# Issuing the stores of k and z from ScalarE instead of from the sync queue

## The chip, the cores and the metric

The kernel runs on one core of a Trainium2 chip. A core has five engines that run their own instruction streams in order: TensorE (PE, with its weight loads PEld), VectorE (DVE), ScalarE (ACT), GpSimd (POOL) and SyncE (SP). SP, ACT and POOL can issue DMAs; 16 DMA engines carry them. The metric is the device time of one execution in microseconds (us), lower is better. Times are the median of several runs; the profile is of one more execution.

## The reference

The input x has shape (8, 3136, 256), in float32. The first block is the real part of a two-dimensional Fourier transform over sequence and features; the second is an MLP with a SoLU activation and a layer norm, over all 25088 tokens.

```python
X = np.fft.fft(x, axis=1)
X = np.fft.fft(X, axis=2)
x = X.real.reshape(B * S, D)
h = x @ w_in                                   # 256 -> 1024
e = np.exp(h - h.max(-1, keepdims=True))
solu = h * e / (e.sum(-1, keepdims=True) + 1e-9)
mu, var = solu.mean(-1, keepdims=True), solu.var(-1, keepdims=True)
out = ((solu - mu) / np.sqrt(var + 1e-6) * g_ln) @ w_out   # 1024 -> 256
```

## The kernel before

**The transform.** The sequence of 3136 is taken as 49 x 64. Batches go in four pairs. For each pair, `load` brings x and its mirrored rows (an indirect DMA from POOL), `add_mirror` and `fold` use the symmetry, and `transform1` does the transform over 49 on PE. ScalarE copies its result from PSUM into z (L154); after every second of these copies a store takes z to a DRAM scratch zd (L156), 8 stores a pair. `turn` reads zd back in another order as g, by four DMAs from POOL each time (L163). `transform2` (L174, L176) does the transform over 64 for one frequency k1, and `take2` copies the result into q (L182).

**Units.** A unit is one k1 of one pair; there are 25 per pair, 100 in all. A unit makes 128 rows of the output for k1 and, by symmetry, 128 for the mirrored frequency 49-k1; both are called signs, 0 and 1 (the first unit of a pair has sign 0 alone). In a unit: `up` multiplies q by the first weight (PE, L200); `even` and `join` make h and its maximum (VectorE); `expo` takes the exponential (ScalarE, L225); `product` multiplies (VectorE, L233) and POOL makes the negative mean (L235); `square` sums the squares (ScalarE, L242); `turn_blocks` transposes u in blocks of 32 x 32 into v (VectorE, L269); `stats` makes the scale (POOL).

**Moves.** The blocks must also change places between partitions. `move_blocks` does that with 16 DMAs on the sync queue, from v to uT (L278), once for a *batch* of two units, at the end of its odd unit. v and uT have two buffers each. This document calls them moves 0 to 15 of a batch; batch n has units 2n and 2n+1.

**Down and store.** `down` multiplies uT with the second weight (PE, L284), three units later (`lag = 3`): the first unit of batch n is multiplied in unit 2n+3, the second in 2n+4. It reads what all 16 moves write. ScalarE scales the result into ot (L290, four buffers). The rows of sign 0, the *store of k*, go out by a plain DMA (L296), those of sign 1 by an indirect DMA from POOL (L293).

**Order.** The loop over units is written by hand, and each engine and queue runs its instructions in that order. PE has up, transform2 of the next unit, transform1 of the next pair (units 4 to 19 of a pair, in the first three pairs), and down. ScalarE has q of the next unit, exp, z (if there is one), squares, ot. The sync queue has, at the end of an odd unit, the store of k of the old unit and then the 16 moves, then loads of x; z's store is issued in between, in units with odd k1.

**Completion counters.** The framework adds the waits. For DMAs issued by SP and ACT it keeps eight completion counters, DMAHW0 to DMAHW7, and gives them out in turn, in the one planned order in which it lists the instructions of all engines. A DMA waits until the DMA that had its counter before has landed.

The lines of the loop that set the order:

```python
            if old:
                store(old, 0, ps_o[0])
            if cur:
                if last:
                    move_blocks(batch, slice(cur.w, cur.w + 1))
                elif cur.w:
                    move_blocks(batch, slice(0, 2))
                stats(cur)
            if ahd:
                ahead(ahd, cur.k1)
            if old and 1 in old.signs:
                store(old, 1, ps_o[1])
```

Of the kernel before, what the change touches and what calls it, by code (L numbers as in the profile page):

```python
# [23 lines left out]
CH = 4  # L24
# [9 lines left out]
def kernel(  # L34
# [19 lines left out]
    nc = tc.nc  # L54
# [9 lines left out]
    out_k = out.rearrange("(p k2 k1) d -> p k1 k2 d", p=NP, k1=N1)  # L64
# [68 lines left out]
    def transform1(pr, s):  # L133

        c, l = divmod(2 * s, CH)
        if s == 0:
            pr.zd = dram.tile([ZR, NH, D], FP32, tag="zd", name="zd")
        if l == 0:  # L140
            pr.z = zpool.tile([ZR, CH, D], FP32, tag="z", name="z")
        y = pr.y[c]
        ps = ps_m.tile([P, 2, D], FP32, tag="m", name="ps1")
        if s == NH // 2 - 1:
            parts = [(ps[0:ZR, 0], y[:, l], 0), (ps[0:ZR, 1], pr.y0[:, 0], 1), (ps[0:ZR, 1], y[:, l + 1], 2)]
        else:
            parts = [(ps[0:ZR], y[:, l : l + 2], 0)]
        first = True
        for o, i, t in parts:
            for h, cs in enumerate((EVEN, ODD)):  # L150
                nc.tensor.matmul(o[..., cs], F[:, 2 * t + h, :], i[..., cs], start=first, stop=True,  # L151
                                 skip_group_check=True)
                first = False
        nc.scalar.copy(pr.z[:, l : l + 2, :], ps[0:ZR])  # L154
        if l == CH - 2:
            nc.sync.dma_start(out=pr.zd[:, c * CH : (c + 1) * CH, :], in_=pr.z)  # L156

    def turn(pr, i):

# [127 lines left out]
    def store(t, s, ps):  # L287

        ot = fpool.tile([P, D], FP32, tag="ot", name="ot", bufs=4)
        nc.scalar.mul(out=ot, in_=ps, mul=t.rs[:, s : s + 1])  # L290
        if s:
            i = NP * NC + t.p * (NK - 1) + t.k1 - 1
            dma = nc.gpsimd.indirect_dma_start(  # L293
                out=out, out_offset=bass.IndirectOffsetOnAxis(ap=idx[:, i : i + 1], axis=0), in_=ot, in_offset=None)
        else:
            dma = nc.sync.dma_start(out=out_k[t.p, t.k1], in_=ot)  # L296

        tc.declare_no_dep(dma.ins, group=f"out{1 - s}", reason="other rows of the output")
        tc.add_to_no_dep_group(f"out{s}", dma.ins)
# [106 lines left out]
    def ahead_pe(pr, step):  # L406

        if 0 <= step - 4 < NH // 2:
            transform1(pr, step - 4)
        elif step - 4 >= NH // 2:  # L410
            turn(pr, step - 4 - NH // 2)

    with tc.manual_schedule():
# [18 lines left out]
        for i in range(len(units) + lag):  # L432
# [26 lines left out]
            if old:  # L459
                store(old, 0, ps_o[0])  # L460
# [8 lines left out]
            if old and 1 in old.signs:  # L469
                store(old, 1, ps_o[1])  # L470
# [76 lines left out]
```

## Time and profile before

| | |
|---|---|
| median of 3 runs | 1433.51 us (1429.29 to 1437.84) |
| profiled execution | 1439.43 us, span 1437.7 us |
| mean granted TensorE clock | 0.923 |
| matmuls busy | 1234.3 us, 86% of the span |
| VectorE, ScalarE, GpSimd busy | 960.4, 615.1, 557.0 us |
| SP's and GpSimd's DMA queues | 58.1% and 9.9% of 16 engines' span |
| ScalarE's DMA queue | 1.7% |

The span is the profiled time from the first to the last instruction. "Busy" leaves out waits and the issuing of DMAs. Of a group of instructions the profile gives line, engine, operation, tiles and count, then the busy time and the mean duration in ns, then the idle time of the engine before them with what ended most of it. A name with a q (SPq) is an engine's sequencer, which waits and issues DMAs. In the list of waits each line has who waited, for whom, the microseconds in total, how often and the longest. In the timeline each line has start, duration, engine, line, operation and how many were merged.

### The profile page before, as it was taken

Reading aid. Unit: us, or ns where it says so; the run is one execution under the profiler, and the core shown is the slowest. Engines: PE = TensorE matmul, PEld = TensorE weight load, DVE = VectorE, ACT = ScalarE, POOL = GpSimd, SP = SyncE. Lnnn points to the kernel's source line nnn. Section 1 sums busy time; section 2 is a strip of 40 time slices with the busy share of each in tenths; the row PEclk is TensorE's granted clock in tenths of the full one; section 3 lists DMA queues with packets and bytes.
Section 4 is the critical chain, followed back from the end, with each engine's and each line's share of the span. In section 5 each row is a group of like instructions: output and inputs, shape, how many; then the busy total and the mean of one; then the engine's idle time right before and its main releaser. Section 6 shows DMA issues by size and latency. Waiting matters only on the chain.

```text
span 1437.7 us, 15866 instructions
## 1 busy us (share of the span) xinstructions
PE 1234.3 (86%) x4864; PEld 929.4 (65%) x4864; DVE 960.4 (67%) x1481; ACT 615.1 (43%) x1149; POOL 557.0 (39%) x972
## 2 busy tenths in 40 slices
PE   1633599999988899999977999999998898898888
PEld 1412376767766677777755777767676576776667
DVE  2597877667765767777656667767765856675671
ACT  1100445445543545554434355545543544454452
POOL 3430435444343444443344345444442323332331
PEclk9566899999999999999989999999999899999998
DMA  9640497795878758786688597886868557465564
GB/s 246 200 97 0 84 159 153 143 166 114 147 147 149 146 122 162 157 158 118 137 142 162 89 171 140 152 153 123 153 125 140 94 97 120 83 113 101 103 116 89
DMA packets 464628, 189.53 MB, mean 132 GB/s; under 512 B 433206, under 2 KB 446782, under 8 KB 464288
## 3 DMA queue, kind: packets, MB, share of 16 engines
q1 hardware_dynamic: 444752, 144.45, 58.1%
q0 software_dynamic: 13824, 38.55, 9.9%
q10 hardware_dynamic: 5968, 5.52, 1.7%
q8 instruction: 40, 0.66, 0.2%
q14 instruction: 44, 0.36, 0.1%
HBM read 44.78 MB, written 38.80 MB: 58 GB/s over the span
## 4 chain that ended last, share of the span: by engine, by line
PE 58%; SPq 15%; DVE 10%; DMA 9%; ACT 3%; issue 3%; POOL 2%; POOLq 0%; DVEq 0%; ACTq 0%
PE ps_o L284 37%; PE ps_h L200 16%; SPq L278 15%; DMA out_dram<-ot 4%; DMA uT<-v 3%; DVE h L214 2%; PE ps L151 2%; DMA xa<-in_x_dram 2%; DVE ex L312 2%; PE ps L174 2%; ACT h L242 1%; ACT u L225 1%; DVE u L233 1%; POOL nmean L235 1%; DMA xb<-in_x_dram,idx 1%
## 5 line engine op out<-in xcount | busy, mean ns | idle before, releaser
L284 PE MATMUL ps_o<-Wo,uT 128*128 128x256 f32 x3136 | 743.5, 398 | 100.4 <-DMA out_dram<-ot 58.1
L284 PEld LDWEIGHTS ps_o<-Wo,uT 128*128 128x128 f32 x3136 | 641.1, 206 | 181.9 <-issue 107.8
L200 PE MATMUL ps_h<-Wi,q 128*128 128x512 f32 x800 | 363.4, 597 | 7.4 <-DVE ev L206 6.4
L233 DVE SCALAR_TENSOR_TENSOR u<-h,u 128x1024 f32<-128x1024 f32 x196 | 232.5, 1223 | 139.2 <-ACT u L225 139.2
L235 POOL TENSOR_SCALAR nmean<-usum 128x1 f32<-128x1 f32 x196 | 128.7, 657 | 505.1 <-DVE u L233 504.9
L225 ACT ACTIVATE u<-h,neg 128x1024 f32<-128x1024 f32 x196 | 223.5, 1141 | 192.9 <-DVE neg L219 192.9
L242 ACT ACTIVATE h<-u,nmean 128x1024 f32<-128x1024 f32 x196 | 223.8, 1143 | 124.3 <-POOL nmean L235 124.3
L214 DVE CUSTOM_DVE_ANT_0 h<-ev,ps_h 128x1024 f32<-128x1024 f32 x196 | 231.7, 1219 | 50.4 <-PE ps_h L200 49.4
L206 DVE SCALAR_TENSOR_TENSOR ev<-w_mid,q,ps_h 128x1024 f32<-128x1024 f32 x100 | 127.8, 1278 | 202.4 <-PE ps_h L200 202.1
L200 PEld LDWEIGHTS ps_h<-Wi,q 128*128 128x128 f32 x800 | 152.8, 191 | 157.8 <-issue 148.4
L269 DVE STREAM_TRANSPOSE v<-u 128x1024 f32<-128x1024 f32 x200 | 238.5, 1234 | 0.1
L182 ACT COPY q<-ps 128x257 f32<-128x257 f32 x100 | 37.4, 374 | 257.7 <-PE ps L176 254.9
L293 POOL DMA_INDIRECT out_dram<-ot,idx x96 | 103.1, 1074 | 113.1 <-ACT ot L290 91.1
L290 ACT ACTIVATE ot<-ps_o,rs 128x256 f32<-128x256 f32 x196 | 83.6, 460 | 121.1 <-PE ps_o L284 121.1
L151 PE MATMUL ps<-y,F 98*100 98x258 f32 (+3 forms) x288 | 81.7, 424 | 42.4 <-DVE y L113 42.4
L254 POOL TENSOR_SCALAR v<-ssq 128x2 f32<-128x2 f32 (+1 forms) x100 | 27.8, 278 | 169.7 <-ACT h L242 169.7
L174 PEld LDWEIGHTS ps<-T,g 128*128 128x128 f32 x400 | 60.4, 191 | 47.4 <-issue 47.4
L151 PEld LDWEIGHTS ps<-y,F 98*100 98x100 f32 x288 | 48.7, 193 | 56.4 <-DVE y L113 25.5
L120 POOL TENSOR_TENSOR xa<-xa,xb 98x1020 f32<-98x1020 f32 (+1 forms) x32 | 72.8, 2274 | 25.4 <-DMA xa<-in_x_dram 16.7
L257 POOL TENSOR_TENSOR rs<-v,neg_half 128x2 f32<-128x2 f32 (+1 forms) x100 | 72.1, 721 | 7.8
L174 PE MATMUL ps<-T,g 128*128 128x128 f32 x400 | 60.7, 274 | 0.0
L163 POOL DMA_DIRECT2D g<-zd x80 | 47.9, 608 | 20.6 <-DMA zd<-z 11.6
(53 smaller groups left out, 492.9 us busy)
## 6 DMA issues: line engine op xcount, KB each, us to landing
uT<-v SPq DMA_DIRECT2D x784, 128.0 KB
zd<-z SPq DMA_DIRECT2D x32, 400.0 KB
g<-zd POOLq DMA_DIRECT2D x80, 160.0 KB, 5.1
out_dram<-ot SPq DMA_DIRECT2D x100, 128.0 KB
xa<-in_x_dram SPq DMA_DIRECT2D x32, 392.0 KB
raw_in_moe_w_in_dram<-in_moe_w_in_dram ACTq DMA_DIRECT2D x1, 2048.0 KB
raw_in_moe_w_out_dram<-in_moe_w_out_dram ACTq DMA_DIRECT2D x1, 2048.0 KB
uT<-v SPq DMA_DIRECT2D x32, 64.0 KB
```

Source lines behind the costliest of these rows:

```text
L151: nc.tensor.matmul(o[..., cs], F[:, 2 * t + h, :], i[..., cs], start=first, stop=True, skip_group_check=True)
L174: nc.tensor.matmul(ps[:, h * P : (h + 1) * P], g[:, k, h * P : (h + 1) * P], T[:, k1, :], start=(h == 0), stop=True, skip_group_check=True)
L200: nc.tensor.matmul(ps[:, fs], t.q[:, c * P : (c + 1) * P], Wi[:, c, fs], start=True, stop=True)
L206: nc.vector.scalar_tensor_tensor(out=t.ev, in0=w_mid, scalar=t.q[:, KD * P :], in1=ps, op0=ALU.mult, op1=ALU.add)
L214: nc.vector.tensor_tensor_reduce(out=t.h[s], in0=t.ev, in1=ps, scale=1.0, scalar=-3.0e38, op0=ALU.subtract if s else ALU.add, op1=ALU.max, ...
L225: nc.scalar.activation(out=t.u[s], in_=t.h[s], func=ACT.Exp, bias=t.neg[:, s : s + 1], accum_out=t.esum[:, s : s + 1])
L233: nc.vector.scalar_tensor_tensor(out=t.u[s], in0=t.h[s], scalar=1.0, in1=t.u[s], op0=ALU.mult, op1=ALU.mult, accum_out=t.usum[:, s : s + 1])
L235: nc.gpsimd.tensor_scalar(out=t.nmean[:, s : s + 1], in0=t.usum[:, s : s + 1], scalar1=-1.0 / FF, scalar2=None, op0=ALU.mult)
L242: nc.scalar.activation(out=t.h[s], in_=t.u[s], func=ACT.Square, bias=t.nmean[:, s : s + 1], accum_out=t.ssq[:, s : s + 1])
L269: nc.vector.transpose(out=t.batch.v[:, t.w, :, o], in_=t.u[s])
L278: nc.sync.dma_start(out=uT[b, i], in_=v[a, q])
L284: nc.tensor.matmul(ps, uT[:, c, :, s], Wo[:, c, :], start=(c == 0), stop=(c == KF - 1))
```

## The change

The two stores are issued by ScalarE's queue, each directly behind the ScalarE instruction that makes its data: z's store behind the copy of z, and the store of k behind the scaling into ot. Nothing else is edited. The engines' compute instructions and POOL's DMAs keep their order; 32 stores of z and 100 stores of k leave the sync queue, which keeps the moves and the loads of x.

```diff
         nc.scalar.copy(pr.z[:, l : l + 2, :], ps[0:ZR])
         if l == CH - 2:
-            nc.sync.dma_start(out=pr.zd[:, c * CH : (c + 1) * CH, :], in_=pr.z)
+            nc.scalar.dma_start(out=pr.zd[:, c * CH : (c + 1) * CH, :], in_=pr.z)
...
         else:
-            dma = nc.sync.dma_start(out=out_k[t.p, t.k1], in_=ot)
+            dma = nc.scalar.dma_start(out=out_k[t.p, t.k1], in_=ot)
```

## The prediction

> **What bounds the kernel now.** I read the page's shares first: TensorE (PE) is busy 86% of the span, VectorE 67%, ScalarE (ACT) 43%. Then the costliest groups and the chain that ended last:
>
> ```profile
> PE 1234.3 (86%) x4864; PEld 929.4 (65%) x4864; DVE 960.4 (67%) x1481; ACT 615.1 (43%) x1149; POOL 557.0 (39%) x972
> ...
> PE 58%; SPq 15%; DVE 10%; DMA 9%; ACT 3%; issue 3%; POOL 2%; POOLq 0%; DVEq 0%; ACTq 0%
> ...
> L284 PE MATMUL ps_o<-Wo,uT 128*128 128x256 f32 x3136 | 743.5, 398 | 100.4 <-DMA out_dram<-ot 58.1
> ```
>
> PE rules, but before its down matmuls (L284) it stands idle 100.4 us, and SP's issuing of moves is on the chain. The SP queue's own waits name what holds it:
>
> ```profile
> SPq L296 <- ACT ot L290: 388.8, 61, 12.9
> SPq L156 <- ACT z L154: 106.4, 21, 7.9
> SPq L278 <- DVE v L269: 88.5, 1, 88.5
> ```
>
> SP waits for ot 61 times and, after the first batch, never for v: at odd units the store of k stands ahead of the batch's 16 moves and holds them. The timeline shows one batch, SP first, then PE:
>
> ```profile
> 1282.36 0.34 SPq L296 DMA_DIRECT2D out_dram<-ot  x1
> 1282.80 13.74 SPq L278 DMA_DIRECT2D uT<-v  x16
> 1296.65 10.86 SPq L296 DMA_DIRECT2D out_dram<-ot  x2
> 1307.61 13.09 SPq L278 DMA_DIRECT2D uT<-v  x16
> ...
> 1291.39 3.60 PE L200 MATMUL ps_h<-Wi,q 128*128 128x512 f32 x8
> ...
> 1300.27 9.82 PE L284 MATMUL ps_o<-Wo,uT 128*128 128x256 f32 x32 [4.72 <-issue]
> 1309.92 3.60 PE L200 MATMUL ps_h<-Wi,q 128*128 128x512 f32 x8
> ...
> 1313.94 7.16 PE L284 MATMUL ps_o<-Wo,uT 128*128 128x256 f32 x32
> 1320.94 3.60 PE L200 MATMUL ps_h<-Wi,q 128*128 128x512 f32 x8
> ```
>
> I write U for the start of a unit's up (L200). An undisturbed unit takes 11.0 us (1309.92 to 1320.94) and down begins at U+4.0. With transform1 in the unit (16 of the 25 units of three pairs) these are 11.85 and 4.9 (timeline around 268 us). The batch of units 2n and 2n+1 is transposed by U+12.4 of its odd unit (1269.36 to 1281.80), stored k leaves at U+13.0, moves at U+13.4, and PE wants uT in the next odd unit, at U+22.0+4.0. Moves need about 16 us to land, so PE comes 3 to 5 us early in about every second batch, and the cold array then takes 9.8 instead of 7.2 us. Wait and cold time together I call the batch's excess. Period of two units less 22.0 (23.7 with transform1) gives it now: 3.9 us in the last pair (U 1034.6 to 1372.0, 13 batches), 1.5 in the first and third pairs' transform1 stretches (175.4 us for 7, 202.3 for 8), 0.8 in the second's (171.8 for 7), 4.5 in the nine batches between.
>
> **What the Trainium skill says.** DMA: Bandwidth & Descriptors, "Issuing engines are not separate DMA queues": other issuers use the same 16 engines and save only the sequencer's time. The page agrees that bytes don't change; SP's ring has 58.1%. Same page, "Why a DMA increments its semaphore by 16 and not by 1": only the full count says that data landed. Perfetto Trace Analysis, "DMA Instruction — HWDGE (DVE, Sync)": the descriptor generator is locked for one DMA, and its sequencer is free afterwards. No stretch of this trace has ACT issue small stores beside SP's moves. TensorE: Matmul & The Clock Gate, "What's actually happening": after an idle window of about 3.4 us the array runs at half rate; the 9.82 beside 7.16 us agrees.
>
> **What decides it: eight completion counters.** The program as built gives hardware DMAs (SP's and ACT's together) eight counters in turn, in the framework's planned order over all engines; a DMA waits until the one before it on its counter has *landed*. On one queue such a wait is on something issued earlier on the same queue. With k on ACT the planned order interleaves, and a move takes a counter from a store. From the changed program, batch 3 (third row is SP's move 13 of 0..15):
>
> ```
> ACT L290 Activation ot_1265<-ps_o_1236,rs_1012 128x256 [waits DMAHW7_49,PE_49]
> ACT L296 DMACopy out_0_dram<-ot_1265 128x256 [waits DMAHW3_49,Activation_49]
> SP  L278 DMACopy uT_1026<-v32_1025 32x16x64 [waits DMAHW3_49]
> ```
>
> ot_1265 is made in the *even* unit after the batch's odd unit, a whole unit after its v. So the last moves of each batch wait for that store: from move 13 or 14 on in batches 1-8, 13, 19, 24-33, and move 15 alone in the rest (9-12, 14-18, 20-23, 34-48). Before, that store simply queued behind the moves.
>
> **The change part by part.** *Removed:* SP's hold at odd units, 0.9 us (U+13.4 against U+12.45), up to 4 us more where ot itself was late. SP loses 132 issues of about 0.35 us, no cover needed.
> *Added on ACT:* 100 stores x 0.36 us and 32 z stores x 0.31 us (SP's own median durations) = 46 us. Covers: ACT idles 254.9 us before q over 93 waits, 2.7 each; h waits 124.3 us for nmean, which hides z. Behind a k store stand ot of sign 1, q and the next exp; q is ready at U+15.4, exp at U+17.5, ACT is through with the first two at U+13.8. So 0 us, until a store holds ACT beyond about 3.5 us.
> *Moved past other queues:* z leaves SP and meets the same cover; its landing of 3.6 us delays the next batch's first move by about the 1 us that was won, where a counter ties them. POOL keeps its order. In the prologue every load still waits for its fold (x loads leave at 38.5, 40.0, 46.2, 52.5, as folds end): 0.
> *Added wait, the largest term.* In the even unit, starting U': store leaves U'+13.0, lands after L, then the gated moves, then PE 0.25 later. L is not shown for ACT. The landing records of SP's k stores give 1.71 us (median, rings empty) and 3.9 (behind moves); I take 2.0, as the earlier moves have mostly landed by then. A move lands 2.66 us after its issue into empty rings, 3.7 to 4.1 in a train; I take 2.9, for the scatter of k's mirror is under way. Three gated moves add two issues of 0.62.
> Sum for one gated move: 13.0+2.0+2.9+0.25 = U'+18.15. PE wants it at 11.0+4.0 = U'+15.0 (11.85+4.9 = 16.75 with transform1). Waits: 3.15 us without transform1; 1.4 with it; 2.65 with it and three gated moves. Cold time after such waits, from the down durations of before (none up to 1.7 us, 1.3 on average near 2.3, 2.5 from 3.9): 1.7, 0.2, 1.4. New excess against old: 4.85-3.9 = 0.95 x 14 batches = 13; 4.05-1.5 = 2.55 x 16 = 41; 1.6-0.8 = 0.8 x 8 = 6; the nine others 4.85-4.5 = 0.35 x 9 = 3. Sum +63 us.
> Both ends: with 1.71 and 2.66 the waits are 2.6, 0.9, 2.1 and the sum about +20 us; with 3.9 and 4.1 they are 6.2, 4.5, 5.7 and the sum about +260. What is late next: the whole following unit, since up stands behind down on PE; the wait repeats in every batch, where now it comes in every second one.
>
> The profiled execution took 1439.4 us (span 1437.7); +63 makes 1502. The median shown, 1433.5, is 0.4% below the profiled one, so I forecast 1495.
>
> **Rivals.** *Freed moves win.* Moves start with v and land at U+12.45+16 = U+28.5. PE wants them at U+26.0 without transform1 (a wait of 2.5 us in one batch of two or 1.3 in each, with cold time an excess near 1.7) and at U+28.6 with it (none): 2.2 x 14 + 1.5 x 16 + 0.8 x 8 + 2.8 x 9 = 86 us less, 1350 us; half of it 1390. For it: 388.8 us of SP's waits vanish. Against: from U'+13.0 to U'+15.0 only 2.0 us remain for a store and a move that take 4.4 into empty rings. It decides only if the last moves don't wait for the store's landing.
> *ACT is held.* A store meets SP's 16 moves and the locked generator. One move's turn (0.6 to 0.9 us) hides. Beyond 3.5 us exp, v and the moves are late: a hold of 5 us costs 1.5 x 48 = 72 us more, 1565 us. For it: T's issues held ACT 8.3 and 5.1 us in the prologue. Against: those have 1600 small rows, k has 128.
> *Nothing measurable:* gains at odd units equal losses at even ones, 1434 us. It needs less than the +20 us of empty rings.
>
> **How the numbers follow.** About 0.5%, 7 us, is what a measurement of this kernel can tell from no change. Gated last moves, likeliest: 0.64, its own range 1450 to 1570. ACT held: 0.13. Freed moves: 0.13. Nothing: 0.10, of which I give 0.02 to slower. So faster 0.13, same 0.08, slower 0.79. The range 1420 to 1580 leaves out most of the full win below (0.09) and the worst of landing times and holds above (0.10).
>
> **What would show it.** Right: SP's waits for ot at L296 are gone, and SP waits 2 to 4 us per batch at L278 for a landing of out_dram<-ot; the train of moves begins within 0.2 us of v, and has a gap before its last one or three; L284's idle time rises from 100 to about 130 or more, with more durations near 9 us; ACT's k stores stay below 1.3 us. Wrong: an unbroken train of moves (freed moves), or ACT's issues of several us with u<-h late behind q (ACT held). The prediction fails most easily on the landing time of a store on ACT's ring: each us is about 45 us of the whole.

## The result and the profile after

The changed kernel takes 1522.26 us (median, 1518.97 to 1527.91), the kernel before, run beside it, 1435.67 us (1429.29 to 1439.85). The ratio is 1.0611 with the interval [1.0558, 1.0664]. The profiled span is 1517.2 us against 1437.7, which is 79.5 us more. The forecast was 1495 us, 1420 to 1580, slower.

The page of the changed kernel first: busy shares, the chain that ended last by engine, and down's group, which has its idle time behind the second bar.

```profile
PE 1252.8 (83%) x4864; PEld 940.4 (62%) x4864; DVE 964.5 (64%) x1481; ACT 624.0 (41%) x1149; POOL 556.8 (37%) x972
...
PE 53%; DVE 15%; DMA 13%; issue 7%; ACT 5%; SPq 4%; POOL 2%; DVEq 0%; POOLq 0%; ACTq 0%
...
L284 PE MATMUL ps_o<-Wo,uT 128*128 128x256 f32 x3136 | 764.1, 406 | 158.4 <-DMA uT<-v 80.1
```

PE's matmuls are busy 18.5 us longer and stand 58.0 us longer ahead of down (158.4 against 100.4); these two make 76.5 of the 79.5 us. The busy times of VectorE, ScalarE and GpSimd moved by less than 10 us each. SPq has fallen from 15% of the chain to 4%: SP no longer issues late, but what it waits for lands late. Its waits (for whom, sum, times, longest):

```profile
SPq L278 <- DVE v L269: 365.9, 37, 96.1
SPq L278 <- DMA out_dram<-ot: 216.7, 44, 9.1
SPq L278 <- DMA zd<-z: 121.4, 17, 11.5
```

The 388.8 us of waiting for ot at L296 are gone. Moves now wait for v, as one would wish; but 44 times a move waits until a store of k has landed, and 17 times until a store of z has. The timeline shows such a batch of the last pair: SP's first fifteen moves, ScalarE's store of k in the even unit, the sixteenth move (move 15), and on PE the start of the even unit, the start of the next and down.

```profile
1327.97 13.14 SPq L278 DMA_DIRECT2D uT<-v  x15
...
1342.28 0.34 ACTq L296 DMA_DIRECT2D out_dram<-ot  x1
...
1344.01 0.58 SPq L278 DMA_DIRECT2D uT<-v  x1
...
1329.34 3.60 PE L200 MATMUL ps_h<-Wi,q 128*128 128x512 f32 x8
...
1340.36 3.60 PE L200 MATMUL ps_h<-Wi,q 128*128 128x512 f32 x8
...
1347.15 8.84 PE L284 MATMUL ps_o<-Wo,uT 128*128 128x256 f32 x32 [2.63 <-issue]
1355.83 3.60 PE L200 MATMUL ps_h<-Wi,q 128*128 128x512 f32 x8
```

The even unit began at U' = 1329.34. Its store left at U'+12.93 and landed, by the landing records, at 1343.88, 1.61 us later. Move 15 was issued at 1344.01 and landed at 1346.95; PE began at 1347.15, after 2.63 us of waiting, and then ran down in 8.84 instead of 7.16 us. Before the change PE waited like this in about every second batch; now it does in nearly every one. The trace shows the cause in all of them: in batches 1 to 48 a late move has its counter from the even unit's store, in 40 of them it leaves within 0.06 us of that store's landing (seven of the other eight lie in the second pair, where z holds moves too), and in all 48 the landing of move 15 is the last of the batch, 0.1 to 0.5 us before down begins.

### The profile page after: what moved, and what is told of

Same layout as the page of the kernel before. It is cut to its first block, busy times and chain, and to the rows that moved or that the text cites. A ratio compares the mean times of both kernels' runs of the same rounds, so it can differ in the third digit from the quotient of the medians.

```text
span 1517.2 us, 15758 instructions
## 1 busy us (share of the span) xinstructions
PE 1252.8 (83%) x4864; PEld 940.4 (62%) x4864; DVE 964.5 (64%) x1481; ACT 624.0 (41%) x1149; POOL 556.8 (37%) x972
## 4 chain that ended last, share of the span: by engine, by line
PE 53%; DVE 15%; DMA 13%; issue 7%; ACT 5%; SPq 4%; POOL 2%; DVEq 0%; POOLq 0%; ACTq 0%
PE ps_o L284 36%; PE ps_h L200 15%; DMA uT<-v 7%; DVE h L214 6%; SPq L278 4%; DMA out_dram<-ot 2%; DVE u L233 2%; ACT u L225 2%; ACT h L242 2%; DMA xa<-in_x_dram 2%; DVE ex L312 2%; DMA zd<-z 2%; POOL nmean L235 1%; PE ps L174 1%; PE ps L151 1%
## 5 line engine op out<-in xcount | busy, mean ns | idle before, releaser
L284 PE MATMUL ps_o<-Wo,uT 128*128 128x256 f32 x3136 | 764.1, 406 | 158.4 <-DMA uT<-v 80.1
L284 PEld LDWEIGHTS ps_o<-Wo,uT 128*128 128x128 f32 x3136 | 653.4, 210 | 250.0 <-issue 141.8
L290 ACT ACTIVATE ot<-ps_o,rs 128x256 f32<-128x256 f32 x196 | 91.4, 466 | 201.6 <-PE ps_o L284 152.0
L151 PE MATMUL ps<-y,F 98*100 98x258 f32 (+3 forms) x288 | 77.5, 408 | 44.6 <-DVE y L113 44.6
L163 POOL DMA_DIRECT2D g<-zd x80 | 47.3, 603 | 13.6 <-issue 13.4
```

Source lines behind the costliest of these rows:

```text
L284: nc.tensor.matmul(ps, uT[:, c, :, s], Wo[:, c, :], start=(c == 0), stop=(c == KF - 1))
```

## The experiments

Ratios are to the kernel before, measured beside each version. "Batch n waits" is PE's idle time directly before down of unit 2n; its sum over 49 batches is 100.4 us before and 154.3 us in the changed kernel. The theory is that of the prediction: a move waits for the landing of a store that has the same completion counter (*tie*). The rivals are that issuing costs ScalarE or the rings time of its own, and that z is to blame rather than k.

**One store at a time.** Only k on ScalarE:

```diff
-            dma = nc.sync.dma_start(out=out_k[t.p, t.k1], in_=ot)
+            dma = nc.scalar.dma_start(out=out_k[t.p, t.k1], in_=ot)
```

> The stores of k alone on ScalarE's queue; z stays on the sync queue. Counter theory (a move waits for the landing of the store that had its completion counter): in the built program the store of k made in the even unit gives its counter to move 14 in batches 2 to 9 and 27 to 34 and to move 14 or 15 in nearly all others, so PE waits 2 to 3 us in each batch as in the changed kernel: 1495 to 1525 us, and SP waits some 200 us for landings of out_dram. Rival (the cost is what ScalarE pays for issuing, in proportion to stores): 100 of 132 stores, three quarters of the 87 us lost, about 1500 us. The two agree here; this run only tells whether z matters.

1512.79 us, ratio 1.0525 [1.0486, 1.0564]; the waits sum to 153.3 us.

```profile
SPq L278 <- DMA out_dram<-ot: 273.6, 55, 9.5
```

The stores of k make nearly all of the loss. With z the ratio is 1.0611 [1.0558, 1.0664], so z adds some 9 us, with intervals that just overlap. Only z on ScalarE:

```diff
-            nc.sync.dma_start(out=pr.zd[:, c * CH : (c + 1) * CH, :], in_=pr.z)
+            nc.scalar.dma_start(out=pr.zd[:, c * CH : (c + 1) * CH, :], in_=pr.z)
```

> The stores of z alone on ScalarE's queue; k stays on the sync queue. Counter theory: the planned order is another one, and in it move 15 of batches 2 to 8 and 27 to 33 (and 14 of 26) takes its counter from the z store of the very unit whose down reads the batch. That store is issued 9.2 us after the unit's up starts, lands 3.6 later, the move 2.9 later, and PE wants it at 4.9: a wait of about 11 us and 2.5 cold in 15 batches, some 12 us more than before in each, 180 in all; moves 11 to 15 of batches 14 to 20 wait for z in the even unit, some 15 us more. About 1630 us (1580 to 1680). Rival (ScalarE pays for issuing, in proportion to stores): 32 of 132 stores, about 1456 us; and if ScalarE's idle time covers them, 1436.

1650.54 us, ratio 1.151 [1.1474, 1.1545]: half of the change costs more than twice as much as the whole. In the program as built, move 15 of batches 2 to 8 and 27 to 33 then has its counter from the z that is stored in the very unit in which PE wants the batch, and these batches wait 10.3 to 11.3 us each. SP's waits show both what stayed and what came:

```profile
SPq L296 <- ACT ot L290: 456.6, 61, 11.6
SPq L278 <- DMA zd<-z: 275.2, 24, 15.2
```

The two edits don't add up, because each shifts which DMAs share a counter. No account by work on engines gives this size: 32 issues of 0.31 us moved from one queue to another.

**Stores of k by the unit in which they are made.** The changed kernel, with the stores of odd units and z still on ScalarE and the stores of even units back on the sync queue:

```diff
+            odd = (t.p * NK + t.k1 + 3) % 2
-            dma = nc.scalar.dma_start(out=out_k[t.p, t.k1], in_=ot)
+            dma = (nc.scalar if odd else nc.sync).dma_start(out=out_k[t.p, t.k1], in_=ot)
```

> As the changed kernel, but the store of k that is made in an even unit goes back to the sync queue, where it stands behind the batch's moves and ahead of nothing urgent. Counter theory: the late tie is gone; the k store of the odd unit gives its counter to move 9 or 10, which comes after it has landed. Moves start with v, so SP's hold is gone too: about 1350 us (1330 to 1400), faster than both. Rival (ScalarE pays, in proportion): 82 of 132 stores, about 1490 us.

1433.12 us, ratio 0.9982 [0.996, 1.0003].

```profile
SPq L278 <- DMA out_dram<-ot: 7.1, 5, 2.3
```

The loss is gone, as the theory says, but the gain that I expected with it did not come; that is taken up below, under the rival. The same edit with the two queues exchanged:

> As the changed kernel, but the store of k that is made in an odd unit, ahead of the batch's moves, goes back to the sync queue; the even unit's k and all z are on ScalarE. Counter theory: the z store of the reading unit gives its counter to move 15 of batches 2 to 8 and 27 to 33, 12 us more in each of 15 batches as in z_only, 180; elsewhere the even unit's k gates moves 12 or 13 to 15, PE waits near 4.8 us without transform1 in 23 batches (+3.4 each, 78) and 2.4 in 8 (+22): about 1710 us (1640 to 1760). Rival (ScalarE pays, in proportion): 82 of 132 stores, about 1490 us.

1803.62 us, ratio 1.2552 [1.2515, 1.2589].

```profile
SPq L278 <- DMA out_dram<-ot: 237.9, 35, 8.0
SPq L278 <- DMA zd<-z: 174.2, 24, 7.9
SPq L297 <- ACT ot L290: 471.8, 48, 13.7
```

Here the two holds come together: the odd unit's store holds the whole train at L297, and the ties hold its end. Waits are 10.1 to 11.6 us in the batches of the transform1 stretches of pairs 1 and 3, which z ties, 5.1 to 6.1 in most of the last pair. The direction and these waits were near what was expected, the total was about 90 us more: in the second pair the waits were 3.5 to 6.9 us instead of 2.4, and I had counted little cold time, while here all 47 full downs that come first in their batch took over 8.5 us, where 7.16 is the warm time.

**The even unit's store left out** of the changed kernel, so that those rows of the output are missing:

```diff
+            if (t.p * NK + t.k1 + 3) % 2 == 0:
+                return
             dma = nc.scalar.dma_start(out=out_k[t.p, t.k1], in_=ot)
```

> The changed kernel, but the stores of k made in even units are left out, so those rows of the output are not written; all other stores leave from ScalarE. If the wait for the landing of the even unit's store is the cause, nothing gates a batch's last moves and the time falls to that of the kernel with these stores on the sync queue: 1425 to 1435 us, with waits for k's landing at L278 below 20 us in sum (216.7 in the changed kernel). If the loss came from ScalarE's own issuing, half of the k stores are still issued there and about half of the 87 us stays: 1475 to 1490.

1430.25 us, ratio 0.9964 [0.9932, 0.9996].

```profile
SPq L278 <- DVE v L269: 456.7, 37, 95.0
SPq L278 <- DMA zd<-z: 126.0, 16, 15.2
...
SPq L278 <- DMA out_dram<-ot: 9.6, 4, 3.6
```

Waits for a landing of k fall from 216.7 to 9.6 us, and the time falls with them. Next, the odd units' k alone on ScalarE: as in the run with even units' stores on the sync queue, and z back there too:

```diff
-            nc.scalar.dma_start(out=pr.zd[:, c * CH : (c + 1) * CH, :], in_=pr.z)
+            nc.sync.dma_start(out=pr.zd[:, c * CH : (c + 1) * CH, :], in_=pr.z)
```

> Only the odd units' stores of k leave from ScalarE; those of even units and z stay on the sync queue. No move then takes its counter from a store issued late on the other ring, and z no longer ties the moves of the second pair. Counters theory: a little faster than with z on ScalarE too (1433 us), about 1405 us (1395 to 1420). Rival, that z on ScalarE is harmless and any difference to before is noise: 1430 to 1437.

1412.9 us, ratio 0.981 [0.9738, 0.9883]: a part of the change is worth having. This is what moves that start with v bring when no late store ties them: about 2% (1.2 to 2.6% by the interval), not the 6% of the rival.

**Every store on ScalarE, one of them later.** The sharpest test leaves the number of ScalarE's issues as it is and changes only when the even unit's store leaves: behind the next unit's store (`late` issues on ScalarE what is held).

```diff
+            if (t.p * NK + t.k1 + 3) % 2 == 0:
+                held.append((t, ot))
+                return
             dma = nc.scalar.dma_start(out=out_k[t.p, t.k1], in_=ot)
...
             if ahd:
                 ahead(ahd, cur.k1)
+            if i % 2 or not cur:
+                late()
             if old and 1 in old.signs:
                 store(old, 1, ps_o[1])
```

> The changed kernel with every store still issued by ScalarE, but the store of k made in an even unit is issued one unit later, right behind the odd unit's own store. In the planned order the last moves of a batch then share no counter with it; moves 9 and 10 share one with a store that left before them. Counters theory: the loss goes although ScalarE issues exactly as much as in the changed kernel: 1425 to 1440 us, L284's idle time near 100 us. Rival, ScalarE's issuing or the second ring itself costs the time: 1500 to 1525.

1438.4 us, ratio 0.9994 [0.9969, 1.002]. The page's line for down, SP's largest waits and the one for k:

```profile
L284 PE MATMUL ps_o<-Wo,uT 128*128 128x256 f32 x3136 | 745.2, 399 | 104.2 <-DMA uT<-v 74.7
```

```profile
SPq L278 <- DVE v L269: 447.3, 37, 95.0
SPq L278 <- DMA zd<-z: 110.1, 16, 12.9
...
SPq L278 <- DMA out_dram<-ot: 13.2, 9, 4.1
```

SP's waits at L278 for landings of k have fallen from 216.7 to 13.2 us, and the loss of 87 us is gone with them, although all 132 stores are issued by ScalarE. That the tie is the cause, and not ScalarE's issuing or the second ring, is shown by this run.

**A later landing.** The even unit's store leaves from a row in four pieces with gaps (the other rows stay whole):

```diff
-        ot = fpool.tile([P, D], FP32, tag="ot", name="ot", bufs=4)
+        ot = fpool.tile([P, 4, 68], FP32, tag="ot", name="ot", bufs=4)
...
+            ot = ot[:, :, 0:64]
```

> The changed kernel, but the even unit's store of k leaves from a row that is cut into four pieces of 256 bytes with gaps, so that it should land later than 1.71 us after its issue: about 2.7, as a single move with 512 pieces does. Same counters, same order. Counters theory: each us of landing costs about 45 us of the whole, so about 1565 us (1545 to 1595), with the median wait before down longer by the same 1 us. Rival, the landing doesn't set the end: 1515 to 1530.

1537.43 us, ratio 1.0697 [1.0638, 1.0756]. The test failed to be one: the store landed after 1.98 us in the median instead of 1.71, not after 2.7. At 45 us for each us that is 12 us, and the ratio rose by 0.0086, also 12 us, within the intervals. But the waits of the last pair stayed at 2.5 to 2.9 us in most batches. The price per us stays unmeasured.

**PE wants the blocks a unit later.** Down four units behind up, in the kernel before and in the changed one:

```diff
-        lag = 3
+        lag = 4
```

> The kernel before with down, and so the store, four units behind up instead of three: PE wants the moved blocks 11 to 12 us later. If landings of moves set PE's waits, nearly all of the 100 us of idle time before L284 and about 40 us of cold time go: about 1300 us (1280 to 1340). If PE's waits are set by something that shifts along with down, the time stays above 1400.

1300.97 us, ratio 0.9045 [0.9001, 0.9089]; the best version of the study.

```profile
L284 PE MATMUL ps_o<-Wo,uT 128*128 128x256 f32 x3136 | 699.5, 381 | 5.2 <-issue 2.8
```

Of 100.4 us of idle time 5.2 are left, and the busy time falls by 44.0 us because the array stays warm: no first down of a batch is over 8.5 us, where there were 18. So the landing of moves was what bound the kernel before, and some 137 us was what it cost.

> The changed kernel with down four units behind up. The landing of the even unit's store and a gated move together take 4 to 6 us after that store; with 11 to 12 us more before PE wants uT nearly all of that is hidden. Counters theory: within 20 us of the four-unit kernel with all stores on the sync queue, about 1315 us (1285 to 1340). Rival, that the stores cost ScalarE or the rings time of their own: the difference between the two stays near 87 us.

1529.82 us, ratio 1.0669 [1.0599, 1.0739]: no gain at all, against my forecast of 1315. I had thought a tie fixed in time while PE's need moved. It moved too. In the last pair of this program as built move 9 has its counter from the even unit's store, and move 15 has one from the store of the *next* odd unit, again one unit before PE wants the batch.

```profile
SPq L278 <- DMA out_dram<-ot: 371.9, 68, 11.0
SPq L278 <- DMA zd<-z: 227.1, 22, 16.4
```

```profile
1315.23 0.34 ACTq L296 DMA_DIRECT2D out_dram<-ot  x1
...
1316.95 0.58 SPq L278 DMA_DIRECT2D uT<-v  x1
...
1320.32 8.84 PE L284 MATMUL ps_o<-Wo,uT 128*128 128x256 f32 x32 [2.87 <-DMA uT<-v]
```

The store landed at 1316.93, the last move left 0.02 us later and landed at 1320.19. With four units the same stores on ScalarE cost 229 us. Next, the tied stores were put off by a unit, as above, but behind exp of the next unit (and the very last store of k is left out):

```diff
+            if (t.p * NK + t.k1 + 4) % 2 == 1:
+                held.append((t, ot))
+                return
...
                 expo(cur)
+            if i % 2 == 0 or not cur:
+                late()
```

> Four units between up and down, every store on ScalarE, and the store that shared its counter with a batch's last move issued in the next unit behind exp, ahead of the next batch's moves. No late move shares a counter with a late store. Counters theory: the time of the four-unit kernel with all stores on the sync queue, 1301 us (1290 to 1320), against 1530 with the tie. Rival, stores on ScalarE cost by themselves: 1400 or more.

1418.75 us, ratio 0.9882 [0.9817, 0.9946]: half of the 229 us is back, not all. In the last pair, which stores no z, nearly all waits are gone: its 24 units take 262.0 us, with the stores on the sync queue 260.9. In the other pairs PE still waits, and the timeline names z:

```profile
273.64 0.31 ACTq L156 DMA_DIRECT2D zd<-z  x1
...
277.29 2.62 SPq L278 DMA_DIRECT2D uT<-v  x4
...
285.49 8.84 PE L284 MATMUL ps_o<-Wo,uT 128*128 128x256 f32 x32 [4.10 <-ACT u L225]
```

z landed at 277.27, and the move with its counter left at 277.29. The name that the profile gives for PE's wait (u, long done) is not the one that ended it; what it read last was the last move of this train, which landed at 285.29. It took 6.0 us to land; this wait is one of three over 4 us in the transform1 stretches of pairs 1 and 3, the 13 others are 1.3 to 3.1 us. Last, the same with z on the sync queue (and no store left out):

> As the last one, four units between up and down, all stores of k on ScalarE, those that shared a counter with a last move issued one unit later, but z back on the sync queue. In the run before it a move waited for z's landing in every batch of the transform1 stretches (z issued 273.6, landed 277.3, move issued 277.3), while the last pair, which has no z, had no wait. Counters theory: without z's ties the time is that of the four-unit kernel with all stores on the sync queue, 1301 us (1290 to 1320). Rival, the stores of k on ScalarE cost by themselves in the stretches where x loads and the scatter run beside them: 1360 to 1420.

1338.36 us, ratio 0.9293 [0.922, 0.9366]. The first and third pairs' transform1 stretches take 379.4 us, with z on ScalarE 436.8, with all stores on the sync queue 378.5: putting z back takes away all of the excess there. 37 us remain, 39.7 by the spans, and the time lies between what the theory and its rival forecast. 12.4 of these lie after the last up, where PE waits 7.7 and 5.1 us, 10.4 in batches 14 to 21, and 14.7 in batches 34 to 47 and the nine between. Loads of x, too, stand behind landings of k now:

```profile
SPq L278 <- DMA out_dram<-ot: 190.7, 31, 9.7
...
SPq L98 <- DMA out_dram<-ot: 120.7, 16, 9.6
```

What these loads, the ties that are left and a cost of the stores themselves have of the rest was not tested.

## Why the prediction was right, and where its sum was off

**The mechanism.** The prediction said that the last moves would wait for the landing of a store made a unit after their data, at about U'+15. The batch shown above has U'+12.93 for the store (13.0 predicted), 1.61 us for its landing (2.0; the median of all even units is 1.71, its own lower end), 2.94 for the move (2.9), and PE waits 2.63 (3.15). By the semaphores in the trace, the stores of k hold just those late moves that the prediction lists, batch by batch. Putting the store off by one unit takes all of the loss away, so this is shown. The Trainium skill (DMA: Bandwidth & Descriptors, "Why a DMA increments its semaphore by 16 and not by 1") says that only the full count means that all data has landed; the trace agrees, with moves that leave 0.02 us after the landing of the store ahead of them on their counter.

**The sum by stretches.** I sum the periods from U of unit 2n+3 to U of unit 2n+5 over the prediction's groups of batches:

| batches | predicted | before, us | after, us | measured |
|---|---|---|---|---|
| 1 to 8 and 26 to 33 (transform1, pairs 1 and 3) | +41 | 403.8 | 442.0 | +38.2 |
| 14 to 21 (transform1, pair 2) | +6 | 197.4 | 225.3 | +27.9 |
| 34 to 47 (no transform1) | +13 | 359.5 | 370.0 | +10.5 |
| nine between | +3 | 243.7 | 241.7 | -2.0 |
| ahead of them and after the last up | 0 | 233.3 | 238.2 | +4.9 |
| sum | +63 | 1437.7 | 1517.2 | +79.5 |

Three groups are within 5 us. **The mis-sized term is the eight batches of the second pair**, "1.6-0.8 = 0.8 x 8 = 6": they lost 3.5 us each. It took one gated move of 2.9 us for them, and allowed for z only at a batch's first move. In the timeline of one of them, the last four moves, a load of x, POOL's load of mirrored rows and PE's down:

```profile
637.50 2.67 SPq L278 DMA_DIRECT2D uT<-v  x4
640.26 1.30 SPq L98 DMA_DIRECT2D xa<-in_x_dram  x1
...
637.47 1.11 POOL L100 DMA_INDIRECT xb<-in_x_dram,idx  x1 [0.23 <-issue]
...
645.58 10.12 PE L284 MATMUL ps_o<-Wo,uT 128*128 128x256 f32 x32 [5.68 <-DMA xa<-in_x_dram]
```

(xa, again, is not what down reads; move 15 landed at 645.23.) A pair has 25 units, so in the second pair z and the loads of x fall into the other parity. The counter of z holds moves from 12 or 13 on, so that four or three are late instead of one. Where z lands early (batches 14, 16, 18 and 20), the wait is 0.8 to 1.5 us, as the forecast of 1.4 has it. In the other four z lands later, the moves leave 1.5 to 1.7 us later, and the wait is 3.3 to 5.8 us. There the last moves are also slow to land: 4.9 to 5.7 us after their issue in batches 15, 17 and 21, against 2.5 to 3.5 in the others.

The load of x directly behind them does not explain that: it stands as close behind the last move in batches 2 to 6 and 27 to 31, which landed in 3.1 to 3.5 us. What batches 15, 17 and 21 have and those do not is a load by POOL issued 0.8 to 2.0 us ahead of the last move (the mirrored rows at L100, in batch 21 g at L163). With k alone on ScalarE, where z holds no late move, such a load leaves 0.2 to 0.7 us ahead of the last move of batches 14 to 18 too: it lands 4.4 to 4.9 us after its issue (3.4 to 3.7 in batches 19 to 21, which have no such load near it), and the stretch takes 231.5 us. That POOL's load slows them is read from this coincidence, and no run separated it. With k's ties gone and z still on ScalarE this stretch takes 213.3 us, with z on the sync queue as well 192.2, so both ties have a share.

The run with the late store takes as long as the kernel before by a balance: by the spans of the same groups, the second pair is 15.9 us longer, where z still holds moves, the last pair 11.2 and the nine batches between 10.1 us shorter, where moves start with v.

**What it would show, point by point.** Waits at L296 gone: yes. SP's waits for landings of k of 2 to 4 us a batch: they are 4.9 us on average, since SP stands earlier at the gated move; the size has no effect on PE. Moves start with v: yes, 37 waits end with v, and the first move leaves within 0.1 us of it, except where z's landing holds this move or a load of x ahead of it (0.6 to 1.4 us), and in one more batch (0.4). Idle time of L284 at 130 or more: 158.4. More downs near 9 us: 30 of 47 first downs of a batch are over 8.5 us, 18 before. ScalarE's stores of k below 1.3 us: 0.34 to 0.37, so *ACT is held* is out, and the run with the late store says so again.

**The rival with the other sign** was out for the reason given, but its price was wrong. It put the free train at 86 us less; without ties it was 1412.9 us, 26 us of span less. In the last pair 14 batches gained 13.6 us where the rival had 2.2 for each, 31 us. Its step "PE wants them at U+26.0 without transform1 (a wait of 2.5 us in one batch of two" is what failed: from batch 40 on that wait is 3.1 to 3.6 us in every second batch, against 3.9 to 4.7 before. Starting the train 0.9 us sooner takes about that much off the wait, and the cold time stays in most of them. The stretches of pairs 1 and 3 gained 7.2 us where the rival had 24, the nine batches 7.2 where it had 25.

## What to carry to other kernels

Moving a DMA to another engine's queue can join two queues that were apart, where the framework's completion counters are shared: look, in the program as built, which DMA had each late transfer's counter before, and how late that one is. A transfer that is off everybody's path becomes critical by being the predecessor of one that is on it. Here, where the kernel waited for transfers, giving them more time (one unit more between up and down took 9.6% off) was worth more than issuing them a little sooner (1.9%).

## What the runs showed of the hardware that was not expected

Over the downs of 32 matmuls in all runs, a wait of PE below 1.47 us left down at 7.15 us. Between 1.47 and 3.7 us it took 7.15 us or 8.5 to 10.2, for waits that differ by hundredths (2.52: 7.15; 2.54: 8.84); all waits above 3.7 us cost 1.4 to 3.0 us. The Trainium skill (TensorE: Matmul & The Clock Gate, "What's actually happening") gives one idle window of about 3.4 us for the clock to fall, with a window that runs freely. The chance in the middle agrees with such a window; that 1.5 us can be enough does not follow from it, and here the measurement decides.

A store of 128 rows of 1 KB landed 1.71 us after ScalarE issued it in even units, where few moves are in flight, and after 2.80 us in odd units, beside the train of moves (medians); z, 400 KB, took 3.64 in the median and up to 12.6.

In the changed kernel the last move of a batch landed 2.6 to 3.5 us after its issue in 41 of 48 batches, in 14 of them with a load of x issued directly behind it. In the other seven it took 4.3 to 5.8 us; these are the ones in which POOL had issued a load 0.7 to 2.0 us ahead of it.
